# A fused attention and feed-forward kernel: scaling weight blocks in pairs, buffers per half-group, and another hand-written order

## The chip, the cores and the metric

The kernel runs on one core of a Trainium2 chip. The metric is the device time of one execution in microseconds (us), the median of several runs. The core has these engines, each with a queue of its own that it works off in order: TensorE (PE, matrix products; its weight loads are listed as PEld), VectorE (DVE), ScalarE (ACT), GpSimd (POOL) and SyncE (SP, which here only issues DMAs). An engine waits for another by semaphores. Numbers that matmuls accumulate lie in PSUM, the rest in SBUF, which has 128 partitions.

## The reference

Four batches, eight heads, 768 positions, head size 64: attention in which a position sees the 8 global positions and the 96 before it, with a linear bias, and then a feed-forward layer on its 3072 rows of 512. In short:

```python
scores = q @ k.T / 8                       # q, k, v: 4 x 8 x 768 x 64
keep = (col < n_global) | ((0 <= row - col) & (row - col < n_local))
scores = where(keep, scores - slope[head] * dist, -1e9)
a = exp(scores - max); a /= sum(a) + 1e-9
x = (a @ v) laid out as 3072 x 512
h = x @ w_in                               # w_in: 512 x 2048, float64
sp = max(h, 0) + log1p(exp(-abs(h)))
out = (h * erf(sp)) @ w_out                # w_out: 2048 x 512, float64
```

The two weight matrices come as 64-bit floats, and the kernel turns them into numbers of 16 bits itself.

## The kernel before

**Precision.** Each operand of a large matmul is held as two 16-bit halves, a high and a low one (hi, lo), and a product is three matmuls: hi by hi, hi by lo, lo by hi. So that the halves fit, a block of weights, and the values v of a batch, are first scaled by a power of two. It comes from the block's largest squared norm: matmuls of the block with itself (a gram block), the maximum of each row (`gram_max`), a matmul with a matrix of ones that sums these over partitions (`sums`), and four short DVE instructions that make the power of two and its inverse (`pow2`).

**Tiles.** The 3072 rows are 24 tiles i of 128, of which a batch b has six. Two tiles make a block u of 256 rows for the feed-forward layer. Its 2048 inner columns are two groups of 1024, so there are 24 groups n = 2u + g. The elementwise work on a group goes in two halves k of 1024 elements per partition: H holds the scaled inner values, A the tanh and its logarithm, B and C further intermediate values, g the two 16-bit halves for the second product. There are `HB` = 5 buffers for the halves of H, `CB` = 3 for A (each of a whole group), 2 each for B and C, 4 for g. The raw blocks of w_out borrow buffers of A, B, C and g before the groups need them.

**The order.** All of it is written out in a table `ORDER` of 2103 steps (line 69). The program issues the instructions of each step in turn, so every engine and the DMA queue work through their parts of the table in this order. Nothing else moves an instruction. A step is a name, its indices and often a letter for the engine (a ACT, v DVE, p POOL). Without a letter the kind has a fixed engine. The names that this text uses:

- Weights: Wd loads a block n = 0..7 of w_in, Wi Wa Wc Wb convert it from 64 bits (Wi mostly on ACT, Wc and Wb, the bitwise steps, on DVE), Wq the gram block, Wr its maximum, Wm the ones matmul, Wp the scale, Wh Wl the high and low half. Rd, Ri, Ra, Rc, Rb, Rq, Rr, Rm, Rp, Rh, Rl are the same for w_out, with 16 rows of blocks and four gram blocks. vd, vq, vm, vp load v and make its scale.
- Attention, tile i: pn a part of the penalties; TK and TQ transpose keys and queries on PE, K and Qc copy them from PSUM; S the scores of four heads on PE; E adds the bias and finds the row's least value (DVE); X the exponential (ACT); eP transposes on PE (early tiles) or et by DMA (later ones), eh and el the high and low half (a cast and a subtraction); V the weighing of the values on PE; x the division by the sums; xh, xl, xt the halves of x and their turning; vh, vl, va halves of v.
- Feed-forward, group n, half k: h the first product, H its scaled copy, t, l, i, G on ACT (tanh, two logarithms, exponential, gelu), P and Q multiplies on DVE or POOL, c and C the two combining steps on DVE, g and j the high and low half, d the second product (eight parts, 0 to 7, each six matmuls of 512 columns), O its scaled copy, o the store.

ACT holds one of two tables of functions, and `act` (line 887) loads the other one when tanh or gelu follows a logarithm or exponential, or the other way.

The lines that the change replaces in the scaling of w_in are these: one maximum per block, one scale per block.

```python
a1 = self.a1[name] = self.small.tile([P, 1], F32, tag="a1", bufs=4, name=f"a1_{name}")
...
self.pow2(f"wi{n}", to=[z[:, n : n + 1] for z in self.s_wi])
```

In the traces nearly every instruction of a step has line 195, that of the helper that records it. So rows are told apart by the names of their tiles: wo also serves as the place of raw w_in blocks, wi_hi and wi_lo are the halves of w_in, kTp and qTp transposed keys and queries in PSUM, kT and qT their copies, s scores, e exponentials, mn row minima, w and eT their halves, po the weighed values, gr_wi a gram block, a_wi its maxima, pt_wi the sums, ex_wi, swi, iwi the scale, h and H, A, B, C, g as above, o the second product's sums.

Of the kernel before, what the change touches and what calls it, by code (L numbers as in the profile page):

```python
# [11 lines left out]
F32 = mybir.dt.float32  # L12
# [9 lines left out]
P = 128  # L22
# [13 lines left out]
HB = 5  # L36
CB = 3
# [32 lines left out]
pn2v TK0 vd0,1,3 pn1a K0a Wd1 Wi0a pn5v ld1,0 KC0,0p Wa0a TQ0 Wc0 Qc0a Wb0 pn3p Wi1a S0,0 TK1 Wq0 E0,0,1 vd0,0,3  # L70
vq0,1,3 ld1,1 vd0,2,3 Wa1a Wr0v pn0p X0,0,1 Wc1 vq0,2,3 E0,0,0 Wm0 K1v vq0,0,3 Rd0 Wb1 TQ1 ld2,0 S0,2 ld0,2 Wq1 pn6a
Qc1a Wp0 ld1,2 vm0 Rd2 pn4p pn7p eP0,0,1 E0,2,1 KC0,1p X0,0,0 E0,2,0 vp0 Ri2p S1,0 eh0,0,1v eP0,0,0 Wh0a el0,0,1 vh0a
Wr1a X0,2,1 TK2 ld2,1 X0,2,0 eP0,2,1 K2a TQ2 E1,0,1 eh0,0,0a Wd2 vl0 KF3p eh0,2,1v E1,0,0 Wd3 Rd4 el0,2,1 S1,2 el0,0,0
eP0,2,0 V0,0 Wl0 ld3,0 Rd5 X1,0,1 eh0,2,0a Ri0a Ra2v E1,2,0 eP1,0,1 el0,2,0 Rd3 Wm1 Wi2v V0,2 Wd4 eh1,0,1a vh1a ld3,1
E1,2,1 Ra0v Rc2 Wa2v X1,0,0 Ri5p Ri3p eP1,0,0 Rd1 Qc2a X1,2,0 X1,2,1 x0 Rb2 Wc2 Wb2 eh1,0,0a vl1 S2,0 Wi3a Wq2 el1,0,1
Wr2v Wa3a TK3 eP1,2,0 el1,0,0 Wc3 Wi4p Wp1 Ra5a Wb3 Ra3a xP0 Ri4a vd1,0,6 Rc3 Wm2 Wa4a Wh1a Ra1a Wp2 Wq3 va1 eh1,2,0a
E2,0,1 Wr3v E2,0,0 xh0v X2,0,1 Wc4 S2,2 Rc0 xl0v eh2,0,1a Wl1 X2,0,0 el1,2,0 Wb4 eh2,0,0a eP1,2,1 ld2,2 Wq4 E2,2,1
eh1,2,1a Wm3 Rb0 Ra4a V1,0 Rd6 Wh2a el1,2,1 vh2a Rc5 K3a V1,2 el2,0,1v Rc4 Wp3 el2,0,0p Wl2 Ri1a X2,2,1 x1 Wd5 xP1
Wh3a Wi5p Ri6a Wr4v Wa5a et2,0,1 xh1a TQ3 va2 eh2,2,1a vq1,0,6 E2,2,0 Ra6a Wl3 Qc3v xl1v Rd7 Wm4 Wd7 Rc1 vd1,1,6 vl2
Rc6 Rb1 Rd12 Wc5 h0,0 h0,1 Ri7a Wd6 Rd13 Wb5 Rd14 el2,2,1p Rb6 Wp4 Rb4 Wq5 S3,0 ld3,2 et2,0,0 Ra7a H0,0a Wh4a Wl4  # L80
E3,0,1 Wr5a X2,2,0 vq1,1,6 Rb3 Ri12p h0,2 ld4,0 Wi7a vd1,2,6 E3,0,0 Ra12a Wa7v Wm5 X3,0,0 Rq0 H0,1a et2,2,1 Rd15 Rb5
# [24 lines left out]
et8,0,0 K9v H5,2v d3,1 X8,2,1 G4,0 x7 o0,1 el8,0,1p d3,2 d3,3 S9,0 xt6 eh8,2,1a et8,0,1 j3,1 d3,4 P4,0v vd2,5,6 Q4,0v
c4,0 C4,0 vl8 d3,5 xh7v el8,2,1p G4,1 d3,6 va8 t5,0 d3,7 eh8,2,0v h5,3 el8,2,0v et8,2,1 ld10,1 i4,1 g4,0a TQ10 O1,0v
E9,0,0 E9,0,1 l5,0 xl7p j4,0 H5,3v V8,0 S9,2 xt7 Qc10v X9,0,0 et8,2,0 h6,0 ld10,0 E9,2,0 vq2,5,6 i5,0 X9,0,1 eh9,0,0v
P4,1p G5,0 o1,0 ld11,1 O1,1a V8,2 Q4,1p c4,1 x8 vd3,0,6 h6,2 eh9,0,1v t5,1 d4,0 el9,0,1p xh8a C4,1 ld9,2 et9,0,1 TK10
d4,1 el9,0,0p E9,2,1 K10a g4,1p d4,2 et9,0,0 H6,0a d4,3 P5,0v xl8p h6,1 X9,2,0 X9,2,1 eh9,2,0v H6,2a Q5,0p vh9v va9  # L110
l5,1 S10,0 ld11,0 el9,2,0v eh9,2,1a vl9 E10,0,1 vq3,0,6 et9,2,0 j4,1 el9,2,1p i5,1 X10,0,1 G5,1 h6,3 V9,0 E10,0,0 TQ11
xt8 d4,4 vd3,1,6 H6,3v S10,2 H6,1v P5,1p t6,0 h7,0 h7,2 t6,1 c5,0 X10,0,0 Qc11a ld10,2 et9,2,1 vq3,1,6 eh10,0,1a
eh10,0,0a E10,2,0 l6,0 Q5,1p H7,0v C5,0 g5,0p H7,2v V9,2 el10,0,1v c5,1 E10,2,1 h7,1 vd3,2,6 l6,1 X10,2,1 i6,0 d4,5
TK11 H7,1a el10,0,0v ld12,1 et10,0,1 x9 C5,1 va10 d4,6 K11v xh9a et10,0,0 g5,1v X10,2,0 h7,3 d4,7 eh10,2,1v S11,0 o1,1
j5,0 j5,1 vq3,2,6 vm2 G6,0 el10,2,1p vh10v xl9v eh10,2,0a E11,0,1 xt9 vl10 d5,0 G6,1 el10,2,0p d5,1 d5,2 P6,0v ld11,2
# [92 lines left out]
class Kern:  # L208
# [178 lines left out]
    def wi_sums(self, n):  # L387
        self.sums(self.a1.pop(f"wi{n}"), f"wi{n}")
# [801 lines left out]
```

## Time and profile before

| | us |
|---|---|
| median of three runs (700.65 to 701.38) | 701.26 |
| the profiled execution | 701.05 |
| its span in the trace | 699.0 |
| PE busy | 656.1 |
| ACT busy | 618.2 |
| DVE busy | 598.3 |
| POOL busy | 244.9 |

The profiled execution's time is that of the whole launch; the span goes from the first instruction to the last. Busy time is what an engine spends in instructions. An engine that is not busy either waits for another one or has nothing left. A row of a time line gives, in square brackets, how long its engine was idle before it, and which engine's work ended that. Times in the trace are counted from the start of the span. The first 7 us are the set-up, which the change leaves as it is. The granted clock of PE is at its lower level, half, in some stretches before 130 us, and at its upper one from there to the end.

### The profile page before, as it was taken

Reading aid. Unit: us, or ns where it says so; the run is one execution under the profiler, and the core shown is the slowest. Engines: PE = TensorE matmul, PEld = TensorE weight load, DVE = VectorE, ACT = ScalarE, POOL = GpSimd, SP = SyncE. Lnnn points to the kernel's source line nnn. Section 1 sums busy time; section 2 is a strip of 40 time slices with the busy share of each in tenths; the row PEclk is TensorE's granted clock in tenths of the full one; section 3 lists DMA queues with packets and bytes.
Section 4 is the critical chain, followed back from the end, with each engine's and each line's share of the span. In section 5 each row is a group of like instructions: output and inputs, shape, how many; then the busy total and the mean of one; then the engine's idle time right before and its main releaser. Section 6 shows DMA issues by size and latency. Waiting matters only on the chain.

```text
span 699.0 us, 13913 instructions
## 1 busy us (share of the span) xinstructions
PE 656.1 (94%) x5280; PEld 457.0 (65%) x5280; DVE 598.3 (86%) x1104; ACT 618.2 (88%) x1004; POOL 244.9 (35%) x167
## 2 busy tenths in 40 slices
PE   3856898999999999999999999999999999999996
PEld 2645786775765785775766766776766766667552
DVE  4799889999999889897996899798877899795894
ACT  4876889999998899898999899999989799998880
POOL 3021022254532845443306323571534412425200
PEclk9975989899999999999999999999999999999999
DMA  8986966757456676434353565534445445130000
GB/s 268 272 258 189 294 180 128 153 102 122 114 84 121 152 129 128 107 74 103 87 101 76 122 137 92 136 77 91 91 92 107 91 106 116 28 57 31 0 31 35
DMA packets 201288, 81.74 MB, mean 117 GB/s; under 512 B 186748, under 2 KB 186748, under 8 KB 201212
## 3 DMA queue, kind: packets, MB, share of 16 engines
q1 hardware_dynamic: 201212, 80.77, 51.5%
q8 instruction: 43, 0.70, 0.4%
q14 instruction: 33, 0.27, 0.1%
HBM read 41.95 MB, written 6.29 MB: 69 GB/s over the span
## 4 chain that ended last, share of the span: by engine, by line
PE 44%; ACT 4%; DVE 2%; issue 1%; ACTq 0%
PE o L195 19%; PE h L195 19%; PE s L195 3%; PE po L195 2%; ACT L195 1%; ACT A L195 1%; PE qTp L195 1%; PE kTp L195 1%; ACT B L195 0%; ACT e L195 0%; DVE C L195 0%; DVE A L195 0%; DVE g L195 0%; DVE B L195 0%; ACT C L195 0%
## 5 line engine op out<-in xcount | busy, mean ns | idle before, releaser
L195 PE MATMUL h<-xT,wi_hi 128*128 128x256 f16 x1536 | 263.6, 278 | 2.4 <-DVE xT L195 1.0
L195 PE MATMUL o<-wo,g 128*128 128x512 f16 x1152 | 262.5, 379 | 0.1
L195 PE MATMUL h<-xT,wi_lo 128*128 128x256 f16 x768 | 212.8, 277 | 0.0
L195 PEld LDWEIGHTS <-g 128*128 128x128 f16 x1152 | 110.4, 98 | 121.8 <-issue 3.3
L195 PEld LDWEIGHTS <-wi_hi 128*128 128x128 f16 x1536 | 151.0, 100 | 32.2 <-issue 5.4
L195 POOL TENSOR_TENSOR w<-e,w 128x512 f16<-128x512 f32 (+1 forms) x54 | 76.2, 1414 | 154.1 <-ACT w L195 111.4
L195 ACT ACT_TABLE_LOAD x95 | 121.9, 1283 | 9.1 <-DVE wi_lo L641 7.5
L195 ACT ACTIVATE e<-e,mn 128x256 f32<-128x256 f32 (+1 forms) x192 | 91.9, 480 | 3.2 <-DVE mn L195 2.9
L195 PEld LDWEIGHTS <-wi_lo 128*128 128x128 f16 x768 | 76.4, 100 | 11.3 <-issue 1.3
L195 DVE CUSTOM_DVE_ANT_0 e<-s,pen 128x256 f32<-128x256 f32 (+1 forms) x192 | 68.2, 394 | 15.1 <-PE s L195 10.5
L195 DVE SCALAR_TENSOR_TENSOR C<-A,B 128x1024 f32<-128x1024 f32 x48 | 65.0, 1354 | 8.4 <-POOL B L195 8.1
L195 DVE SCALAR_TENSOR_TENSOR g<-C,gs,g 128x1024 f16<-128x1024 f32 x48 | 67.8, 1415 | 2.8 <-POOL g L195 1.3
L195 DVE SCALAR_TENSOR_TENSOR C<-C,H 128x1024 f32<-128x1024 f32 x48 | 61.7, 1286 | 0.5
L195 PE MATMUL s<-kT,qT 64*128 64x256 f32 (+1 forms) x384 | 57.9, 409 | 4.2 <-DVE mn L195 2.7
L195 POOL TENSOR_SCALAR g<-C,gs 128x1024 f16<-128x1024 f32 x23 | 32.2, 1398 | 84.2 <-DVE C L195 53.3
L195 POOL TENSOR_TENSOR B<-C,B 128x1024 f32<-128x1024 f32 x18 | 47.2, 2621 | 33.2 <-DVE A L195 32.7
L195 POOL TENSOR_TENSOR A<-A,B 128x1024 f32<-128x1024 f32 x15 | 37.5, 2501 | 51.8 <-ACT C L195 44.6
L195 ACT ACTIVATE A<-A,halves 128x1024 f32<-128x1024 f32 x48 | 54.8, 1142 | 0.2
L195 ACT ACTIVATE B<-A 128x1024 f32<-128x1024 f32 x48 | 50.8, 1058 | 4.7 <-DVE C L195 3.1
L195 DVE TENSOR_TENSOR A<-A,B 128x1024 f32<-128x1024 f32 x33 | 41.9, 1269 | 12.3 <-ACT C L195 7.6
L195 ACT ACTIVATE C<-A 128x1024 f32<-128x1024 f32 x48 | 50.5, 1054 | 1.5 <-DVE g L195 1.2
L195 ACT ACTIVATE A<-H 128x1024 f32<-128x1024 f32 x48 | 50.0, 1050 | 1.4 <-DVE H L195 1.0
(141 smaller groups left out, 930.8 us busy)
## 6 DMA issues: line engine op xcount, KB each, us to landing
wo<-in_moe_w_in SPq DMA_DIRECT2D x8, 1024.0 KB
raw_wo<-in_moe_w_out SPq DMA_DIRECT2D x12, 512.0 KB, 7.1
out<-osb SPq DMA_DIRECT2D x24, 256.0 KB, 2.2
kraw<-in_k SPq DMA_DIRECT2D x23, 256.0 KB, 4.6
qraw<-in_q SPq DMA_DIRECT2D x23, 256.0 KB, 3.3
vraw<-in_v SPq DMA_DIRECT2D x23, 256.0 KB, 3.0
va<-vb SPq DMA_DIRECT2D x20, 240.0 KB, 3.7
vm<-in_v SPq DMA_DIRECT2D x18, 256.0 KB, 3.0
```

The source lines that it names most:

```text
L195: i = getattr(self.engine, name)(*a, **k)
```

## The change

Four things.

1. The scale of weight blocks is made for two blocks at once. `gram_max` writes the maxima of two blocks into the two columns of one tile; the ones matmul (Wm, Rm) and the scale (Wp, Rp) then run once for a pair m, on two columns: four and two times instead of eight and four.
2. A tile of A holds half a group, and there are five of them (`CB`) instead of three whole ones. `half` returns the tile of the half. A raw row block of w_out takes one of these tiles instead of half of a whole one.
3. There are six buffers for the halves of H (`HB`) instead of five.
4. The table `ORDER` is a new one throughout (2091 steps). Some steps change engine: of the 48 P multiplies POOL has 13 where it had 15, of the 48 Q 11 where it had 18; of the low halves of the exponentials (el) 44 where it had 54; of their high halves (eh) DVE has 53 where it had 36; of the scaled copies H it has 42 where it had 49.

A step `SS` is added that the table does not use, and the branch for other sizes of n_global and n_local, which does not run here, is fitted to the pairs.

```diff
-HB = 5
-CB = 3
+HB = 6
+CB = 5
...
-pn2v TK0 vd0,1,3 pn1a K0a Wd1 Wi0a pn5v ld1,0 KC0,0p Wa0a TQ0 Wc0 Qc0a Wb0 pn3p Wi1a S0,0 TK1 Wq0 E0,0,1 vd0,0,3
...
+pn1a TK0 K0v vd0,0,3 Wi0a Wa0a TQ0 Wd1 Wc0 Wb0 pn3p Qc0v KC0,0p S0,0 ld1,0 pn2p pn0p ld1,1 pn7a Wi1a E0,0,1 ld1,2 TK1
...
     def gram_max(self, name, z="v"):
 
-        a1 = self.a1[name] = self.small.tile([P, 1], F32, tag="a1", bufs=4, name=f"a1_{name}")
+        kind, n = name[:2], int(name[2:])
+        if (kind, n // 2) not in self.a1:
+            self.a1[kind, n // 2] = self.small.tile([P, 2], F32, tag="a1", bufs=4, name=f"a1_{name}")
+        a1 = self.a1[kind, n // 2][:, n % 2 : n % 2 + 1]
...
-    def wi_sums(self, n):
-        self.sums(self.a1.pop(f"wi{n}"), f"wi{n}")
+    def wi_sums(self, m):
+        self.sums(self.a1.pop(("wi", m)), f"wi{m}")
...
-        self.pow2(f"wi{n}", to=[z[:, n : n + 1] for z in self.s_wi])
-        self.wi_done = n + 1
+        self.pow2(f"wi{m}", 2, [z[:, 2 * m : 2 * m + 2] for z in self.s_wi])
+        self.wi_done = 2 * m + 2
         self.h_scales(0)
...
-        elif b == 0 and c % 2 == 0:
-            t = self.chain.tile([P, 2, 2 * DM], F32, tag="A", bufs=self.cb, name=f"raw_wo_{n}")
-            self.raw_wo[n], self.raw_wo[n + 1] = t[:, 0:1, :], t[:, 1:2, :]
+        elif b == 0:
+            self.raw_wo[n] = self.chain.tile([P, 1, 2 * DM], F32, tag="A", bufs=self.cb, name=f"raw_wo_{n}")
...
     def half(self, n, k):
-        return self.A[n][:, k * HW : (k + 1) * HW]
+        return self.A[n, k]
 
     def tanh_part(self, n, k):
-        if k == 0:
-            self.A[n] = self.chain.tile([P, GW], F32, tag="A", bufs=self.cb, name=f"A_{n}")
+        self.A[n, k] = self.chain.tile([P, HW], F32, tag="A", bufs=self.cb, name=f"A_{n}_{k}")
         self.act(self.half(n, k), self.H[n, k], AF.Tanh, scale=0.5, g=True)
```

**What moves: DVE's first steps after the set-up.** Two penalties, the two bitwise steps of weight block 0 (wo), a bias step of two heads in two instructions each (ISA), the maximum of the gram block, a bitwise step of block 1. Before:

```order
L195 TENSOR_SCALAR pen<-wi_lo 128x384 x2
L195 SCALAR_TENSOR_TENSOR wo<-wo 128x1024 x2
L195 ISA e_0_1_203,mn_176<-s_0_1_184,pen 128x128
L195 ISA mn_176 128x1
L195 ISA e_0_1_203,mn_176<-s_0_1_184,pen 128x128
L195 ISA mn_176 128x1
L195 TENSOR_REDUCE a_wi_215<-gr_wi_194 128x1
L195 SCALAR_TENSOR_TENSOR wo<-wo 128x1024
```

After, where the key and query copies stand here too, and the maximum does not:

```order
L195 COPY kT<-kTp_153 128x4x128
L195 SCALAR_TENSOR_TENSOR wo<-wo 128x1024 x2
L195 COPY qT_175<-qTp_164 128x512
L195 ISA e_0_1_192,mn_173<-s_0_1_179,pen 128x128
L195 ISA mn_173 128x1
L195 ISA e_0_1_192,mn_173<-s_0_1_179,pen 128x128
L195 ISA mn_173 128x1
L195 SCALAR_TENSOR_TENSOR wo<-wo 128x1024
```

The copies kT and qT came from ACT, and the two penalties went to ACT and POOL.

**What moves: the scale on DVE.** Before, the scale of block 0 (ex_wi, swi, iwi) follows a bitwise step of block 1, and bias steps of the second four heads of tile 0 come after it:

```order
L195 COPY kT<-kTp_189 128x4x128
L195 SCALAR_TENSOR_TENSOR wo<-wo 128x1024
L195 TENSOR_SCALAR ex_wi_263<-pt_wi_226 128x1
L195 TENSOR_SCALAR ex_wi_263<-ex_wi_263 128x1
L195 TENSOR_SCALAR swi<-ex_wi_263 128x1
L195 TENSOR_SCALAR iwi<-ex_wi_263 128x1
L195 ISA e_2_1_279,mn_176<-s_2_1_241,pen 128x128
```

After, it is made for blocks 0 and 1 together (128x2), behind these bias steps and behind the maximum of block 1; the softmax halves of tile 0 (eT) stand behind it:

```order
L195 ISA e_2_0_275,mn_173<-s_2_0_237,pen 128x128
L195 ISA mn_173 128x1
L195 TENSOR_REDUCE a_wi_271<-gr_wi_254 128x1
L195 TENSOR_SCALAR ex_wi_293<-pt_wi_281 128x2
L195 TENSOR_SCALAR ex_wi_293<-ex_wi_293 128x2
L195 TENSOR_SCALAR swi<-ex_wi_293 128x2
L195 TENSOR_SCALAR iwi<-ex_wi_293 128x2
L195 CAST eT_0_1_307<-eP_0_1_227 128x2x128
L195 TENSOR_TENSOR eT_0_1_307<-eP_0_1_227,eT_0_1_307 128x2x128
```

So the scale now needs both maxima, and that of block 1 is on DVE just ahead of it.

**What moves: ACT's first steps.** From the copy of the first queries to block 1's conversion, the first exponentials and the sums of squares of v (vm), before:

```order
L195 COPY qT_178<-qTp_170 128x512
L195 ACTIVATE wo<-wo 128x1024
L195 ACTIVATE vm_1_158,a_v_208<-vm_1_158 128x1024
L195 ACTIVATE wo<-wo 128x1024
L195 ACT_TABLE_LOAD
L195 ACTIVATE e_0_1_203,sm_177<-e_0_1_203,mn_176 128x128 x2
L195 ACTIVATE vm_2_212,a_v_208<-vm_2_212 128x1024
L195 ACTIVATE vm_0_206,a_v_208<-vm_0_206 128x1024
L195 ACTIVATE pen<-wi_lo 128x384
L195 COPY qT_259<-qTp_233 128x512
L195 ACTIVATE e_0_0_223,sm_177<-e_0_0_223,mn_176 128x128 x2
```

After, from the first table load on:

```order
L195 ACT_TABLE_LOAD
L195 ACTIVATE e_0_1_192,sm_174<-e_0_1_192,mn_173 128x128 x2
L195 ACTIVATE vm_1_202,a_v_225<-vm_1_202 128x1024
L195 ACTIVATE pen<-wi_lo 128x384
L195 ACTIVATE e_2_1_245,sm_174<-e_2_1_245,mn_173 128x128 x2
L195 ACTIVATE e_0_0_222,sm_174<-e_0_0_222,mn_173 128x128 x2
L195 COPY qT_269<-qTp_230 128x512
L195 ACTIVATE gr_wi_210,a_wi_271<-gr_wi_210 128x256
L195 ACTIVATE vm_2_249,a_v_225<-vm_2_249 128x1024
L195 ACTIVATE vm_0_160,a_v_225<-vm_0_160 128x1024
```

The maximum of the gram block of weights 0 (gr_wi, a_wi) is now on ACT, behind six exponentials of tile 0 and the query copy of tile 1. On PE, the ones matmul of block 0 (pt_wi) that stood between the first gram block and the queries of tile 1 is gone, and a transposing of exponentials (eP) stands in its place.

## Rows read from the trace of the kernel before

**Rows 1.** The page, first part: busy us, share of the span, instructions.
```profile
PE 656.1 (94%) x5280; PEld 457.0 (65%) x5280; DVE 598.3 (86%) x1104; ACT 618.2 (88%) x1004; POOL 244.9 (35%) x167
```

**Rows 2.** Stretches: start:end, length, busy PE PEld DVE ACT POOL, PE clock, DMA share, GB/s.
```profile
28.00:60.00 32.00, 20.53 (x161) 15.55 (x159) 31.52 (x80) 23.54 (x56) 5.02 (x6) 0.76 0.73 225
60.00:140.00 80.00, 70.18 (x584) 57.11 (x585) 74.23 (x185) 69.70 (x135) 15.57 (x15) 0.82 0.77 193
140.00:215.00 75.00, 74.42 (x637) 51.36 (x635) 72.64 (x134) 74.50 (x133) 34.75 (x24) 1.00 0.56 100
215.00:690.00 475.00, 473.57 (x3825) 321.02 (x3822) 405.12 (x650) 432.26 (x647) 183.46 (x107) 1.00 0.44 91
```

**Rows 3.** DVE's time line, 7 to 28 us: start, us, operation, [idle before].
```profile
11.86 2.67 DVE L195 SCALAR_TENSOR_TENSOR wo<-wo 128x1024 int32<-128x1024 int32 x2 [3.33 <-ACT wo L195]
...
17.41 0.42 DVE L195 TENSOR_REDUCE a_wi<-gr_wi 128x1 f32<-128x256 f32 x1 [2.46 <-PE gr_wi L195]
...
22.39 0.29 DVE L195 CUSTOM_DVE_ANT_0 e<-s,pen 128x128 f32<-128x128 f32 x1 [0.76 <-PE s L195]
...
24.38 0.29 DVE L195 CUSTOM_DVE_ANT_0 e<-s,pen 128x128 f32<-128x128 f32 x1 [1.49 <-PE eP L195]
...
27.68 0.42 DVE L195 CUSTOM_DVE_ANT_0 e<-s,pen 128x256 f32<-128x256 f32 x1 [1.05 <-PE eP L195]
```

**Rows 4.** The time lines of DVE (first row) and PE around 214 us.
```profile
213.84 1.27 DVE L195 SCALAR_TENSOR_TENSOR g<-C,gs,g 128x1024 f16<-128x1024 f32 x1
...
214.94 2.32 PE L195 MATMUL o<-wo,g 128*128 128x512 f16 x10
```

**Rows 5.** The time line of ACT, 7 to 27 us.
```profile
9.67 2.16 ACT L195 ACTIVATE wo<-wo 128x1024 f32<-128x1024 f32 x2
...
14.25 1.13 ACT L195 ACTIVATE wo<-wo 128x1024 f32<-128x1024 f32 x1 [1.94 <-DMA wo<-in_moe_w_in]
...
17.46 1.28 ACT L195 ACT_TABLE_LOAD   x1
...
26.19 0.36 ACT L195 ACTIVATE gr_wi<-gr_wi 128x256 f32<-128x256 f32 x1
```

**Rows 6.** The time line of PE, 7 to 20 us.
```profile
12.36 1.23 PE L195 MATMUL s<-kT,qT 64*128 64x128 f32 x8 [1.42 <-ACT qT L195]
...
17.89 0.59 PE L195 MATMUL pt_wi<-a_wi,ones 128*128 128x1 f32 x2 [0.52 <-DVE a_wi L195]
```

**Rows 7.** DVE by shape: count | busy us, mean ns | idle before.
```profile
L195 DVE SCALAR_TENSOR_TENSOR C<-A,B 128x1024 f32<-128x1024 f32 x48 | 65.0, 1354 | 8.4 <-POOL B L195 8.1
...
L195 DVE TENSOR_SCALAR H<-h,hs 128x512 f32<-128x512 f32 x49 | 36.3, 743 | 4.6 <-PE h L195 4.6
...
L195 DVE CAST w<-e 128x512 f16<-128x512 f32 x29 | 16.5, 570 | 6.5 <-ACT e L195 6.5
...
L195 DVE COPY qT<-qTp 128x512 f32<-128x512 f32 x8 | 5.5, 682 | 0.0
...
L195 DVE TENSOR_SCALAR wo<-raw_wo,swo 128x512 f16<-128x512 f32 x5 | 2.4, 478 | 0.0
...
L195 DVE TENSOR_SCALAR ex_wi<-pt_wi 128x1 int32<-128x1 int32 x8 | 1.2, 148 | 0.0
```

**Rows 8.** The time lines of DVE (two rows) and POOL near 605 us.
```profile
604.59 2.57 DVE L195 CAST w<-e 128x512 f16<-128x512 f32 x1
607.77 0.43 DVE L195 CAST w<-e 128x512 f16<-128x512 f32 x1 [0.61 <-ACT e L195]
...
604.33 2.55 POOL L195 TENSOR_TENSOR A<-A,B 128x1024 f32<-128x1024 f32 x1 [6.07 <-ACT C L195]
```

**Rows 9.** The chain of waits, 353 to 365 us: start, us, engine, operation.
```profile
355.18 0.44 PE qTp L195 x4
...
363.30 0.70 PE po L195 x24
```

More of the change, by code (lines that the diff above doesn't have):

```diff
@@ L481, in weights @@
             self.gram_max(f"wi{n}")
-            self.wi_sums(n)
-            self.wi_scale(n)
-            for part, e in (("h", "a"), ("l", "v")):
-                self.wi_halves(n, e, part)
+            if n % 2:
+                self.wi_sums(n // 2)
+                self.wi_scale(n // 2)
+                for k in (n - 1, n):
+                    for part, e in (("h", "a"), ("l", "v")):
+                        self.wi_halves(k, e, part)
         for b in range(2 * NG):
@@ L491, in weights @@
             self.gram_max(f"wo{b}")
-            self.wo_sums(b)
-            self.wo_scale(b)
-            for n in range(b * HC, (b + 1) * HC):
-                for part, e in (("h", "a"), ("l", "v")):
-                    self.wo_split(n, e, part)
+            if b % 2:
+                self.wo_sums(b // 2)
+                self.wo_scale(b // 2)
+                for n in range((b - 1) * HC, (b + 1) * HC):
+                    for part, e in (("h", "a"), ("l", "v")):
+                        self.wo_split(n, e, part)
     def v_load(self, b, i, k):
@@ L728, in width, with score_tile, score_part @@
         return WIN if i % NT else P
-    def score_part(self, i, p):
+    def score_tile(self, i):
+        self.score_part(i, 0)
+        self.score_part(i, 2, self.ps_h, "h")
+    def score_part(self, i, p, pool=None, tag="s"):
         c, n = self.cs[i], self.width(i)
         c0 = i % KR * KP + PREV + NGL + P - n
-        pss = [self.ps_a.tile([P, 2, WIN], F32, tag="s", bufs=2, name=f"s_{i}_{p}_{j}") for j in range(2)]
+        pss = [(pool or self.ps_a).tile([P, 2, WIN], F32, tag=tag, bufs=2, name=f"s_{i}_{p}_{j}") for j in range(2)]
         for a in range(2):
@@ L1054, in branch @@
             pool = lambda n, b, **k: cx.enter_context(tc.tile_pool(name=f"{n}_{int(fast)}", bufs=b, **k))
[L1055 removed]
+            self.cb, self.hb = (CB, HB) if fast else (2, 2)
             for n in ("pt", "vs", "qT", "us", "vm", "a_v", "gr", "a1", "hs", "h_done", "raw_wo", "raws", "tp", "cs", "va", "vb", "xT", "hp", "H", "A", "B", "C", "g", "pos", "osb"):
@@ L1065, in branch @@
             if not fast:
-                with tc.tile_pool(name="wr", bufs=HC + 1) as self.wr:
+                with tc.tile_pool(name="wr", bufs=2 * HC) as self.wr:
                     self.weights()
```

245 lines of the change are left out of this document (122 added, 123 removed).

## The prediction

> **What bounds the kernel now.** I began with the busy times, then read stretches of the span, then DVE's waits in the order in which they happen. [rows 1] TensorE (PE) is busy 656.1 us of a span of 699.0 and VectorE (DVE) 598.3, so neither is slack. [rows 2] Of the 43 us that PE is idle, little lies late: from 140 to 215 it is busy 74.42 of 75, from 215 to 690 473.57 of 475. The rest lies before 140 us and in the tail. So the end is the moment at which PE has got through the opening, plus PE work that does not change.
>
> What sets that moment is mostly DVE. [rows 3] shows its five waits: 3.33, 2.46, 0.76, 1.49 and 1.05 us, 9.1 us in all, the last ending at 27.7 us. [rows 2] From 28 to 215 us DVE is busy 31.52 + 74.23 + 72.64 = 178.4 of 187: another 8.6 us of idle time, but in small holes. [rows 4] shows how close the two engines are: DVE's low half of the activations for group 3 ends at 213.84 + 1.27 = 215.11 us, and PE's ten down-projection matmuls that begin with this group start at 214.94 (the first two use the high half). PE has no gap there, DVE has none before it. So until about 215 us these two finish together, and **DVE's start plus DVE's work plus its holes up to this point is a floor under the end**. DVE has less work per group behind it (no weights are left to convert): from 215 to 690 it is busy 405 of 475 [rows 2], so it has room later, and what is left is PE's.
>
> So I compare before and after at this one point, the first down matmul of group 3, in four terms: idle time of DVE in the opening, its holes after that, DVE work ahead of the point, PE work behind it.
>
> **Term 1, DVE's opening.** I followed the new rows of DVE, ACT and PE by hand up to 41 us, with the durations of the trace.
> The key copy goes from ACT to DVE, so ACT converts weight block 0 about 0.4 us sooner: before it ends at 9.67 + 2.16 = 11.83 [rows 5], now at 11.4. DVE, done with the key copy at 8.7, waits 2.85 instead of 3.33.
> The query copy (0.68 [rows 7]) also goes to DVE, but behind both bitwise steps of block 0 (2.67 [rows 3]): it ends at 14.65, before at 12.3 on ACT. The scores (1.23 [rows 6]) follow, so the first bias step starts at 16.05: a wait of 1.4 that was not there.
> Block 1 still waits for its load, at 14.25 [rows 5]; DVE converts it to 19.9. Then it needs the second pair of scores, which on PE now stands behind a transposing that needs the first exponential. That one pays the table load of 1.28 [rows 5] and ends near 18.9; the scores end at 21.85. Wait 2.05.
> **The pair.** The scale of blocks 0 and 1 needs both maxima. That of block 1 is on DVE at 23.4 (with 0.15 of waiting). That of block 0 was DVE's first job after the gram matmuls (at 17.41 [rows 3]); now it is on ACT behind two parts of exponentials of tile 0 that wait for DVE at 22.5, and a query copy. It starts at 24.55 and takes 0.36 [rows 5]; the ones matmul takes up to 0.59 [rows 6]. The scale starts at 25.5: DVE waits 2.1. Queued behind it are the transposed softmax parts of tile 0 and the scale of v, for which ACT in turn waits until about 30.4.
> Next, the bias of tile 1 waits for scores that PE could not start before: 1.4. ACT then works off 8.4 us in a row before DVE gets its cast of tile 1: 0.35 and 1.0 lost; and a score pair behind the weighing of tile 0 costs 1.1.
> Sum: 2.85 + 1.4 + 2.05 + 0.15 + 2.1 + 1.4 + 0.35 + 1.0 + 1.1 = 12.4 us against 9.1, so **+3.3 us**. Below, it can be 0: steps of a few tenths may fall together, and before had its last wait at 27.7. Above I take 5, if what ACT owes at 39 us costs another wait of half of the largest in [rows 3].
>
> **Term 2, DVE's holes from 28 to 215 us**, 8.6 us. In a hole DVE waits for ACT, PE or POOL. If DVE comes 3.3 us later and the other engine does not, a hole shrinks by as much as it is long, up to 3.3 us in all; if the other engine was itself waiting for DVE (ACT's exponentials follow DVE's bias steps, PE's transposings follow them), nothing shrinks. From 140 to 215 ACT is busy 74.50 of 75 [rows 2], so it has no room to come earlier; from 60 to 140, where 5.8 of the 8.6 lie, it is busy 69.70 of 80 and PE 70.18, so they have. I take half: **-1.6 us**, bounds 0 and -3.3.
>
> **Term 3, DVE work ahead of group 3.** Counted in both orders. Gone or moved behind: four scalings of w_in with five short instructions and two of w_out with four, at 0.15 each, 3.0 + 1.2 = 4.2 [rows 7]; six high halves of w_out 6 x 0.48 = 2.9; four moves of H 4 x 0.74 = 3.0; one pair of the two steps on C, 1.35 [rows 7] and about the same, 2.6; smaller ones (weight conversions, two penalties, an output, a bias) 4.3. Together 17.0. Added: eleven casts of exponentials at 0.43 when free [rows 8], 4.7; three query and two key copies 5 x 0.68 = 3.4 [rows 7]; three subtractions of about the size of such a copy, 2.0, and smaller ones (integer conversions of w_out, maxima, a penalty) 5.3. Sum 15.4, net **-1.6 us**. The bounds: the 29 such casts of before took 0.570 in the mean [rows 7], which with eleven makes the net 0; -3 if half of the added ones fall into waits.
> The rule to weigh here is one of contention. The rows first: a DVE cast of 0.43 took 2.57 from 604.59, when GpSimd (POOL) was in a multiply of 2.55 from 604.33 [rows 8]. The Trainium skill, "SBUF — State Buffer", section "SBUF: two separate sides", says that the two engines share a port pair that one holds for a whole instruction while the other blocks; by that rule the trace agrees. A sum that let every added cast wait as this one did would be 11 x 2.1 = 24 us; the mean of the 29 says that few do, and the order takes multiplies off POOL (24 of 33 stay there), so I keep the mean as the bound.
>
> **Term 4, PE work.** Behind the point stand one key transposing (0.44, like the query's) and one weighing (0.70) more than before [rows 9]: **+1.1 us**. The six ones matmuls that go lie ahead of the point, under waits of DVE: nothing. The weighing waits for nothing late, so this term is firm to 0.2.
>
> **The rest.** The sixth H buffer and A in five halves take the place of five and three whole ones: 44 KB a partition either way. What they can give is bounded by what PE still loses after 140 us, 0.58 from 140 to 215 and 1.43 from 215 to 690 [rows 2]: 0 to -2.0. I take 0, since a new order brings its own pauses. Loads: SP has weight block 3 behind the low half of v of tile 0, in both orders; that is now some 3 us later, and ACT reaches it at 39.5, when it should be there: nothing, else part of term 1's upper end. The store at the end is the same.
>
> **Sum.** +3.3 - 1.6 - 1.6 + 1.1 = +1.2, on a profiled execution of 701.05 us (a span of 699.0 and 2.05 around it). The median of the three runs is 701.26, so I add there: 702.46, rounded **702.5 us**, 0.2% slower. The terms do not end low together: the holes shrink only as far as the opening is late. With an opening of 0 and no shrinking, 0 - 3 + 1.1 - 2.0 = -3.9 gives 697.4; at the upper ends, 5 + 0 + 0 + 1.1 gives 707.4.
>
> **Rivals.**
> (a) Slower: the holes do not shrink. Then +3.3 - 1.6 + 1.1 = +2.8: 704.1; at the upper ends 707.4. For it: ACT is full from 140 us on [rows 2], and before that its exponentials follow DVE's bias steps, so it is made late by the same waits. Against: PE and ACT are both idle an eighth of 60 to 140 us. It decides if, of the 8.6 us, more than 7 are still there in the profile after.
> (b) Faster: DVE opens no later than before, since waits that I added one after the other overlap, and the buffers take away PE's late pauses: -1.6 + 1.1 - 2.0 = -2.5, 698.8. For it: DVE has 26 steps up to the second bitwise step of block 2 where it had 35, so less stands in front; the late pauses exist. Against: the pair's scale cannot start before ACT's maximum, and ahead of 215 us no buffer is shown to be waited for.
> (c) Slower still, by ACT and DVE in turn. If ACT falls behind in the opening, DVE's multiplies wait for ACT's logs and ACT's logs for B buffers that DVE frees; every exchange carries the lateness on and adds its own latency. At two waits of about 1.5, as the fourth of [rows 3], on top of (a), the end is 707. It decides if DVE's idle time from 60 to 215 us, 8.1 of the 8.6 before, grows by 3.
> (d) The casts behind POOL: four of eleven at 2.1 more is 8.6 us on DVE and 711, and the contention above is its mechanism. The mean of [rows 7] speaks against it.
> That the change does not do what it says (halves of A freed apart, scales in pairs) is ruled out by the rows of the order. That it buys and costs nothing is the lower half of the forecast.
>
> **How the numbers follow.** The forecast, with 700.0 to 704.0 as its own range, 0.42; (a) 0.23; (b) 0.22; (c) 0.09; (d) 0.04. A difference under 0.2% (1.4 us, 699.9 to 702.7) is about what a measurement of this kernel can tell from none. Of the forecast 0.22 lies within it and 0.20 above; (a) to 0.03 within, all the rest of it, (c) and (d) above; (b) to 0.17 below and 0.05 within. So faster 0.17, same 0.30, slower 0.53. The range that leaves out 2 in 10 goes from 697.4, the sum of the low ends, to 707.4, that of the high ones.
>
> **What would show it.** Right: in the profile after, DVE's waits up to 41 us sum to about 12 us, one of some 2 us before the scale of the first pair (ended by the ones matmul), and the holes after that to about 7; the first down matmul of group 3 starts between 215 and 216. Wrong in term 1: that sum is under 10. Wrong in term 2: the holes are as large as before. Wrong in term 3: the casts' mean is far from 0.5. Wrong as a whole: PE pauses for more than 3 us in sum after 220 us; then the floor that I used is not what decides.

## The result, and the profile after

The changed kernel takes 705.28 us (median of five executions: four from 702.69 to 707.19; the fifth, 717.62, was disturbed and is left out of the ratio), against 701.25: the ratio is **1.0058, 95% interval 1.003 to 1.0087**, slower by 0.58%. The profiled execution is the fastest of them, 702.69 us with a span of 700.9.

The page of after, busy time as in [rows 1]: PE 7.6 us less, DVE 19.7 more, POOL 43.1 less.

```profile
PE 648.5 (93%) x5268; PEld 450.8 (64%) x5268; DVE 618.0 (88%) x1118; ACT 612.2 (87%) x985; POOL 201.8 (29%) x143
```

The stretches of after, columns as in [rows 2]:

```profile
28.00:60.00 32.00, 17.75 (x144) 14.07 (x144) 29.26 (x67) 26.11 (x55) 5.73 (x5) 0.71 0.82 255
60.00:140.00 80.00, 65.37 (x578) 53.59 (x579) 76.80 (x173) 66.20 (x135) 17.98 (x16) 0.82 0.74 175
140.00:215.00 75.00, 74.21 (x615) 50.64 (x613) 73.95 (x140) 73.86 (x124) 24.85 (x19) 1.00 0.58 114
215.00:690.00 475.00, 474.27 (x3844) 321.63 (x3841) 422.25 (x685) 429.64 (x640) 147.38 (x87) 1.00 0.43 89
```

From 215 to 690 us PE is as full as before (474.27 of 475), though DVE has 17 us more to do there: that work costs PE no pause.

DVE's waits in after, as in [rows 3]:

```profile
11.35 2.49 DVE L195 SCALAR_TENSOR_TENSOR wo<-wo 128x1024 int32<-128x1024 int32 x2 [2.72 <-ACT wo L195]
...
15.76 0.29 DVE L195 CUSTOM_DVE_ANT_0 e<-s,pen 128x128 f32<-128x128 f32 x1 [1.33 <-PE s L195]
...
20.43 0.29 DVE L195 CUSTOM_DVE_ANT_0 e<-s,pen 128x128 f32<-128x128 f32 x1 [0.86 <-ACT pen L195]
...
23.75 0.16 DVE L195 TENSOR_SCALAR ex_wi<-pt_wi 128x2 int32<-128x2 int32 x1 [2.03 <-PE pt_wi L195]
...
26.38 0.42 DVE L195 CUSTOM_DVE_ANT_0 e<-s,pen 128x256 f32<-128x256 f32 x1 [1.20 <-ACT vm L195]
...
37.45 0.69 DVE L195 TENSOR_TENSOR eT<-eP,eT 128x512 f16<-128x512 f32 x1 [1.14 <-ACT eT L195]
39.43 0.42 DVE L195 CUSTOM_DVE_ANT_0 e<-s,pen 128x256 f32<-128x256 f32 x1 [1.29 <-PE s L195]
```

These are the waits that the prediction walked through, in its order: 2.72 (2.85 was forecast), 1.33 (1.4), 0.86 (2.05), 2.03 for the ones matmul of the pair (2.1), 1.20 (1.4), 1.14 and 1.29. Their sum is 10.6, not 12.4. Two ended otherwise than forecast: this trace puts the 0.86 and the 1.20 down to ACT (a penalty, a sum of squares), where the prediction had scores on PE. The low half for group 3 ended at 215.06, where before had 215.11 [rows 4]:

```profile
213.78 1.28 DVE L195 SCALAR_TENSOR_TENSOR g<-C,gs,g 128x1024 f16<-128x1024 f32 x1
```

In this one execution, then, nothing was lost up to the point, and the 1.6 us by which it is longer than the profiled one of before lie behind it. But the median is 2.6 us above this one. Where that goes is seen in a second trace.

### The profile page after: what moved, and what is told of

It reads as the page before. It is cut to its first block, busy times and chain, and to the rows that moved or that the text cites. A ratio compares the mean times of both kernels' runs of the same rounds, so it can differ in the third digit from the quotient of the medians.

```text
span 700.9 us, 13820 instructions
## 1 busy us (share of the span) xinstructions
PE 648.5 (93%) x5268; PEld 450.8 (64%) x5268; DVE 618.0 (88%) x1118; ACT 612.2 (87%) x985; POOL 201.8 (29%) x143
## 4 chain that ended last, share of the span: by engine, by line
PE 74%; DVE 16%; ACT 4%; issue 2%; DMA 1%; SPq 1%; DVEq 0%; ACTq 0%
PE h L195 31%; PE o L195 30%; PE s L195 5%; PE po L195 4%; DVE wo L195 3%; DVE C L195 2%; DVE raw_wo L195 2%; DVE e L195 2%; DVE w L195 1%; PE kTp L195 1%; DVE g L195 1%; PE qTp L195 1%; DMA qraw<-in_q 1%; DVE A L195 1%; DVE B L195 1%
## 5 line engine op out<-in xcount | busy, mean ns | idle before, releaser
L195 PE MATMUL h<-xT,wi_hi 128*128 128x256 f16 x1536 | 259.1, 275 | 0.0
L195 POOL TENSOR_TENSOR w<-e,w 128x512 f16<-128x512 f32 (+1 forms) x44 | 65.9, 1502 | 167.4 <-DVE w L195 77.8
L195 POOL TENSOR_SCALAR g<-C,gs 128x1024 f16<-128x1024 f32 x20 | 28.7, 1437 | 142.5 <-DVE C L195 64.4
L195 DVE SCALAR_TENSOR_TENSOR C<-A,B 128x1024 f32<-128x1024 f32 x48 | 61.0, 1273 | 0.3
L195 DVE TENSOR_TENSOR A<-A,B 128x1024 f32<-128x1024 f32 x35 | 46.3, 1323 | 6.4 <-ACT C L195 5.1
L195 PEld LDWEIGHTS s<-kT,qT 64*128 64x128 f32 x384 | 35.5, 199 | 25.3 <-issue 9.9
L195 DVE TENSOR_TENSOR B<-C,B 128x1024 f32<-128x1024 f32 x37 | 48.3, 1306 | 3.7 <-POOL A L195 3.3
L195 ACT ACTIVATE B<-B 128x1024 f32<-128x1024 f32 x48 | 50.4, 1052 | 0.4
```

The source lines that it names most:

```text
L195: i = getattr(self.engine, name)(*a, **k)
```

## Experiments

All ratios are to the kernel before on the same chip. Its median was 700.6 to 701.5 there, with single executions from 697.6 to 704.1, so a single trace says little on the total, and much on durations and waits. The rows come from several chips, so they are compared by their ratios rather than by their medians.

| kernel | median, us | ratio, 95% interval |
|---|---|---|
| after, again | 706.00 | 1.0057 (1.0037 to 1.0077) |
| new opening, old rest | 707.96 | 1.0085 (1.0066 to 1.0104) |
| old opening, new rest | 705.46 | 1.0049 (1.0032 to 1.0066) |
| before, A in six halves | 700.79 | 0.9998 (0.9982 to 1.0015) |
| before, DVE late | 704.08 | 1.0057 (1.0035 to 1.0078) |
| before, 36 POOL multiplies | 705.19 | 1.0069 (1.0043 to 1.0095) |
| before, 72 POOL fills | 700.26 | 0.9983 (0.9966 to 1.0001) |
| after, maximum 0 on DVE | 703.58 | 1.0047 (1.0030 to 1.0064) |
| after, load of block 1 first | 703.39 | 1.0052 (1.0030 to 1.0073) |
| after, both of these | 702.51 | 1.0037 (1.0020 to 1.0053) |
| before, load of block 1 first | 698.18 | 0.9966 (0.9952 to 0.9981) |
| after, 15 steps from POOL to ACT | 708.34 | 1.0117 (1.0098 to 1.0136) |

**The changed kernel again** (no edit).

> The changed kernel once more, to see whether its times scatter wider than those of the kernel before (702.7 to 707.2 in four executions, against 700.2 to 701.4). Theory T (a floor set by the opening of VectorE, then TensorE work): the scatter is chance of a few executions, and the median falls near 703, +0.3%. Rival S (something in the new order is sensitive to a quantity that differs from one execution to the next): the median stays near 705, +0.5%, executions lie 3 us and more apart, and a profiled execution differs from the first one (span 700.9) in one stretch.

Rival S on the median: 706.0, though before scatters as widely on this chip. The trace (span 702.8) differs from the first in the opening. The time line of ACT of the first, then of the second, where the first weight block that comes by a later load (block 1) is waited for:

```profile
13.99 2.16 ACT L195 ACTIVATE wo<-wo 128x1024 f32<-128x1024 f32 x2 [2.26 <-DMA wo<-in_moe_w_in]
```

```profile
15.14 2.16 ACT L195 ACTIVATE wo<-wo 128x1024 f32<-128x1024 f32 x2 [3.27 <-DMA wo<-in_moe_w_in]
```

And DVE's time line of the second, three of its eight waits:

```profile
17.34 1.23 DVE L195 SCALAR_TENSOR_TENSOR wo<-wo 128x1024 int32<-128x1024 int32 x1 [0.92 <-ACT wo L195]
...
22.60 0.29 DVE L195 CUSTOM_DVE_ANT_0 e<-s,pen 128x128 f32<-128x128 f32 x1 [1.88 <-PE s L195]
...
29.61 0.43 DVE L195 CUSTOM_DVE_ANT_0 e<-s,pen 128x256 f32<-128x256 f32 x1 [2.07 <-PE s L195]
```

Block 1 landed 1.15 us later, and DVE waited 0.92 for its conversion. The next two waits shown, 0.86 and 1.20 in the first trace, are 1.88 and 2.07. Here are the rows of PE ahead of the first of these, in the first trace, then in the second:

```profile
18.97 0.60 PE L195 MATMUL qTp<-ident,qraw 128*128 128x128 f32 x4
19.50 0.71 PE L195 MATMUL s<-kT,qT 64*128 64x128 f32 x8
```

```profile
20.23 1.06 PE L195 MATMUL qTp<-ident,qraw 128*128 128x128 f32 x4
21.22 1.23 PE L195 MATMUL s<-kT,qT 64*128 64x128 f32 x8
```

The same transposings and scores took 1.0 us longer together, and that is about what the wait grew by. PE's granted clock is on record at its upper level from 17.8 to 24.6 us in the first trace (it fell behind a pause of PE of 2.1 us), and from 29.7 on in the second. Ahead of its rise PE worked without a pause from 14.49 to 17.67 in the first, and paused for 0.45 at 15.86 in the second, for a load. But in a later kernel (after, load of block 1 first) it worked without a pause from 14.71 on, and the upper level is on record from 21.0 only; what decides the moment stays open.

The sum up to 43 us is 13.1, and 13.9 in a third trace of this opening (the next kernel; upper level from 28.7). So 10.6, 13.1 and 13.9, mean 12.5; three traces of the old opening have 9.1, 10.0 and 8.6, mean 9.2.

**New opening with the old rest, and the other way.** The two orders are joined at the first down matmul of group 3. The first kernel has the table of after up to the step d3,0 and then what is left of the steps of before, in the order of before. The second has it the other way round, with A in six halves and H in five buffers.

> The new order up to the first down matmul of group 3 (about 215 us), then the remaining steps in the order of before, with the new kernel's buffers and paired scales. Theory T: that matmul starts at about 215, as in both profiles, and the rest is that of before: 701 to 702, +0.1%. Rival S1 (the scatter arises in the opening, ahead of 215 us): executions 3 us and more apart and a median of 704 to 705. Rival S2 (it arises behind): a tight set near 701.5.

> The order and the scaling of before up to the first down matmul of group 3, then the remaining steps in the new order (A in six half tiles and H in five, since that opening needs them). Theory T: what stands behind the point costs 1.1 to 1.4 us more on TensorE in the new order, so 702.4 to 702.7, +0.2%. Rival S1 (the scatter arises in the opening): a tight set at 702.5 or below. Rival S2: executions 3 us and more apart, median near 705.

Both medians missed theory T, to the slow side; the executions of the second lie within 1.8 us, as S1 has it. The joints have a price of their own: with the old opening the point is reached at 214.8 us, as before, and the last down matmuls start 480.9 us behind it instead of 477.0. Of these 3.9 us, 2.2 are pauses of TensorE between 230 and 245 us; the new rest finds steps done in another order there, and five H buffers instead of six, and which of the two makes the pauses was not tested. So these two don't say what the rest costs. What they give are two more traces of each opening: by the time of the point, the scatter lies ahead of it (S1), since in the unjoined traces the last down matmuls start 478.5 and 478.3 us behind it in after, 477.0 and 477.1 in before and its next variant. That is 1.3 us more in after.

**Before with A in halves.**

```diff
-CB = 3    # whole tiles of A
+CB = 6    # half tiles of A
-        return self.A[n][:, k * HW : (k + 1) * HW]
+        return self.A[n, k]
```

> The kernel before with one edit: each tile of A holds half a group and there are six of them in place of three whole ones, so that halves come free apart; order, scaling and H buffers as before. Theory T: no buffer of A is waited for where it counts, 701.3, within 0.1%. Rival B (the late pauses of TensorE, 0.7 us at 350 to 360 and 0.6 at 530 to 540, are waits for buffers): 699.5 to 700.5, -0.15 to -0.25%.

Theory T: 0.9998, and its trace has both late pauses of PE as before (0.74 and 0.66). They are no waits for A. A sixth H buffer was not tested by itself.

**Before with DVE late.**

```diff
-... Rd0 Wb1 TQ1 ld2,0 S0,2 ...
+... Rd0 Wb1 ZZ12 TQ1 ld2,0 S0,2 ...
```

The step ZZ12 is twelve DVE instructions on a scratch tile of 200 columns.

> The kernel before with twelve short extra VectorE instructions on a scratch tile behind the second bitwise step of weight block 1 (about 21 us), some 3 us in all: only this engine's opening is made late, nothing else changes. The holes of term 2 tell the theories apart. Theory T (half of a late opening is absorbed in later holes, as term 2 has it): the first down matmul of group 3 comes 1.5 us later and the end too: 702.8. Rival F (the waits of the opening are passed on in full): 3 us later, 704.3. Rival N (VectorE's start is no floor): under 0.5 us, 701.5.

The time line of DVE shows that the twelve took more than planned:

```profile
22.06 4.77 DVE L195 SCALAR_TENSOR_TENSOR scr<-scr 128x200 f32<-128x200 f32 x12
...
28.28 0.29 DVE L195 CUSTOM_DVE_ANT_0 e<-s,pen 128x128 f32<-128x128 f32 x1 [0.53 <-PE eP L195]
```

4.77 us were put in, and up to the point DVE is busy 4.1 us more than in the mean of the old opening. The waits of the opening took back 0.8 (8.4 in sum against 9.2), and the idle time from there to the point is 0.3 less. The point came at 217.0, 3.0 later than the mean of 214.9, 214.8 and 212.4. Of these 3.0, 0.6 stood ahead of the twelve: in this trace the wait for the gram block was 3.46 against 2.8 in the mean, so 2.4 are left to them. The median is 3.3 higher (4.0 by the ratio). With what was really put in, T has 2.4 and F 4.8, so neither holds as it stands: **between half and five sixths of a late VectorE is passed on; what is taken back is taken back in the waits of the opening, and the later holes, of which term 2 spoke, shrink by 0.3 us.**

**Before with more work on POOL.** In the three traces of the new opening I took each DVE instruction ahead of 215 us and compared it with the usual length of its shape (the tenth percentile over all traces). Those that are longer by over 0.1 us sum to 9.4, 8.4 and 7.6 us; with the old opening to 6.2, 5.4 and 5.7. Each one of them lies beside an instruction of POOL. The time line of DVE of after shows two of them, at 56.03 and 94.78, and the same two shapes at their usual length, at 94.18 and 54.84:

```profile
54.84 1.28 DVE L195 SCALAR_TENSOR_TENSOR wi_lo<-wo,swi,wi_hi 128x1024 f16<-128x1024 f32 x1
56.03 1.66 DVE L195 SCALAR_TENSOR_TENSOR raw_wo<-raw_wo 128x512 int32<-128x512 int32 x1
...
94.18 0.69 DVE L195 SCALAR_TENSOR_TENSOR raw_wo<-raw_wo 128x512 int32<-128x512 int32 x1
94.78 2.19 DVE L195 SCALAR_TENSOR_TENSOR wi_lo<-wo,swi,wi_hi 128x1024 f16<-128x1024 f32 x1
```

And POOL's time line of the same kernel:

```profile
55.81 1.32 POOL L195 TENSOR_TENSOR w<-e,w 128x512 f16<-128x512 f32 x1 [13.32 <-ACT w L195]
...
94.23 1.66 POOL L195 TENSOR_TENSOR w<-e,w 128x512 f16<-128x512 f32 x1 [14.86 <-ACT w L195]
95.86 2.44 POOL L195 TENSOR_SCALAR wo<-wo 128x512 f32<-128x512 f32 x2
```

A bitwise step of 0.69 takes 1.66, from 56.03: POOL's subtraction ends at 57.13, 1.10 after its start, and it is 0.97 late. Two kernels tell whether that is the cause, and what about POOL's work:

```diff
-... Ri5p Ri3p eP1,0,0 Rd1 ...
+... Ri5p Ri3p ZZ3 eP1,0,0 Rd1 ...
```

The step ZZ3, at twelve places, is three POOL multiplies of 200 columns on a scratch tile.

> The kernel before with 36 short extra GpSimd multiplies on a scratch tile, in twelve groups of three behind its steps between 30 and 115 us; no other engine reads them. In the traces of the changed kernel VectorE's instructions ahead of group 3 are longer by 2 us in sum than in those of before, and each long one lies beside one of GpSimd. Theory C (GpSimd's instructions hold VectorE's up): VectorE's busy time from 28 to 140 us grows by 3 us or more, single instructions by up to the length of a group, and the end comes 2 to 4 us later, 703.5 to 705.5. Rival N (the two only lie beside each other by chance): busy time and end as before, within 0.5 us.

```diff
-            self.nc.gpsimd.tensor_tensor(self.scr, self.scr, self.scr, op=ALU.mult)
+            self.nc.gpsimd.memset(self.scr, 0.0)
```

Here each place has six of them instead of three.

> As the run with 36 extra GpSimd multiplies (end 4.4 us later, the multiplies at 0.51 us when free), but with 72 extra GpSimd fills of the same scratch tile with zeros (0.27 us each), six behind each of the same steps: about as much GpSimd time, of instructions that write and read nothing. It tells what about a GpSimd instruction holds VectorE up. Theory R (an instruction that reads its input from the same memory, as the Trainium skill, page "SBUF - State Buffer", section "SBUF: two separate sides", has it for two-input instructions of VectorE): VectorE's two-input instructions keep their length, and the end is within 1 us of that of before, 700.5 to 701.7. Rival C (any GpSimd instruction): busy time of VectorE from 28 to 140 us grows by 2 or more, 703 to 705.5.

The stretches up to the end of DVE's low half for group 3 (columns as in [rows 2], the third busy time is DVE's), of before, of the one with multiplies, and of the one with fills:

```profile
0.00:215.11 215.11, 179.17 (x1445) 134.63 (x1446) 192.52 (x455) 185.41 (x357) 61.49 (x60) 0.90 0.72 177
```

```profile
0.00:218.78 218.78, 179.62 (x1446) 134.84 (x1446) 197.90 (x455) 186.19 (x357) 92.01 (x97) 0.88 0.70 174
```

```profile
0.00:215.17 215.17, 179.31 (x1445) 134.75 (x1446) 192.47 (x455) 185.91 (x357) 80.87 (x133) 0.90 0.72 177
```

Theory C for the multiplies: DVE has the same instructions and is busy 197.90 instead of 192.52; its over-long ones sum to 11.6; the end is 4.4 us later. Theory R for the fills: 19.4 us more of POOL, DVE at 192.47, the sum 5.7, no difference in time. **So it is POOL's instructions with an input in SBUF that hold VectorE up; the fills, which have none, don't.** Counted over thirteen traces (all but that of the fills), whole spans, instructions that lay beside POOL's for over 0.15 us: of those with all inputs in SBUF, 379 of 793 of the five big multiplies were longer by over 0.1 us; of those with an input in PSUM (bias steps, copies of H, of queries and of outputs, divisions) none of 1769. Who began first decides: of the 793, 454 began while an instruction of POOL was running, and the 379 are all among these; of the 339 beside which POOL's began later, none was longer. The Trainium skill, "SBUF — State Buffer", section "SBUF: two separate sides", has the exclusive port pair only for VectorE's instructions with two SBUF inputs or in a fast mode, and against two inputs only for GpSimd instructions that read SBUF; by these counts, these traces agree.

**After without the wait for the maximum of block 0.**

```diff
-... X0,0,1 E0,0,0 vq0,1,3 ... Qc1a Wr0a Rd2 E0,2,0 ...
+... X0,0,1 E0,0,0 Wr0v vq0,1,3 ... Qc1a Rd2 E0,2,0 ...
```

> The changed kernel with one step moved: the maximum of the gram block of weights 0 is taken by VectorE behind the first half of the bias of tile 0 instead of by ScalarE behind six exponentials, so the pair's scale waits for one maximum only. Theory T: the wait of 2.0 to 2.2 us ahead of the scale of the first pair shrinks to about 0.7, VectorE has 0.4 more to do, and the end comes about 1 us earlier than that of the changed kernel, 704.3 to 705. Rival N (the next wait takes it up): no change, 705.3 to 706.

DVE's time line, the scale of the pair:

```profile
22.79 0.16 DVE L195 TENSOR_SCALAR ex_wi<-pt_wi 128x2 int32<-128x2 int32 x1 [0.48 <-PE pt_wi L195]
```

The wait is 0.48 instead of 2.0 to 2.2: theory T for the wait. For the time it isn't clear of noise: by the ratios the kernel is 0.7 to 0.8 us faster than after, and the intervals overlap.

**The load of block 1 first**, in after and in before.

```diff
-pn1a TK0 K0v vd0,0,3 Wi0a Wa0a TQ0 Wd1 ... S0,0 ld1,0 pn2p ...
+pn1a TK0 K0v Wi0a Wa0a TQ0 Wd1 ... S0,0 ld1,0 vd0,0,3 pn2p ...
```

> The changed kernel with one load moved: the first 512 KB of v are loaded behind weight block 1 and the first keys of tile 1 instead of ahead of them. In three traces of that opening weight block 1 landed at 13.99, 14.49 and 15.14 us, and the sum of VectorE's waits up to 43 us was 10.6, 13.9 and 13.1. Theory L (the landing of block 1 is what lets that opening vary): it lands about 1 us sooner, and the end comes 1 to 2 us earlier, 703.5 to 705. Rival N (ScalarE and TensorE set it all the same): no change, 705.3 to 706.

> The changed kernel with both moves of the opening: weight block 1 and the first keys of tile 1 are loaded ahead of the first 512 KB of v, and the maximum of gram block 0 is on VectorE. Each alone gave 703.4 to 703.6 against 705.3 to 706.0. Theory T (the waits of the opening are passed on, and these two stand in a row): VectorE's waits up to 43 us sum to about 9, the end is at 702 to 702.8. Rival N (both take away the same wait): 703.3 to 703.8.

> The kernel before with the same load moved: weight block 1 and the first keys of tile 1 ahead of the first 512 KB of v, and the sum of squares of that part of v behind block 1's second conversion on ScalarE. Theory T: block 1 lands at about 12.6 instead of 14.3 to 15.0, VectorE's second wait (2.5 to 3.3 us for the gram block) shrinks by about 1, and the end is about 1 us earlier than that of the kernel before: 699.8 to 700.3. Rival N (later waits take it up): 700.8 to 701.3.

In before the edit moves two steps, the load (vd0,1,3) and, on ACT, the sum of squares of that part of v (vq0,1,3), which needs this load:

```diff
-pn2v TK0 vd0,1,3 pn1a K0a Wd1 Wi0a pn5v ld1,0 KC0,0p ... vd0,0,3 vq0,1,3 ld1,1 vd0,2,3 Wa1a Wr0v ...
+pn2v TK0 pn1a K0a Wd1 Wi0a pn5v ld1,0 vd0,1,3 KC0,0p ... vd0,0,3 ld1,1 vd0,2,3 Wa1a vq0,1,3 Wr0v ...
```

ACT's time line of after with the load first, and DVE's time line of before with it:

```profile
12.56 2.17 ACT L195 ACTIVATE wo<-wo 128x1024 f32<-128x1024 f32 x2 [0.62 <-DMA wo<-in_moe_w_in]
```

```profile
15.72 0.42 DVE L195 TENSOR_REDUCE a_wi<-gr_wi 128x1 f32<-128x256 f32 x1 [0.78 <-PE gr_wi L195]
```

512 KB less ahead of it let block 1 land at 12.56 instead of 13.99 to 15.14: theory L for the load. In after the gain in time isn't clear of noise: by the ratios 0.4 us with the load first and 1.4 with both moves, and their intervals overlap that of after. The trace of both has 7.6 us of waits up to 43 us, less than forecast. In before the gain is clear: the wait for the gram block falls from 2.46 [rows 3] to 0.78, the waits after it by another 1.3, and the time by 0.34%, more than T expected: **698.18 us, ratio 0.9966 (0.9952 to 0.9981), the fastest kernel of this study**.

The gram block that DVE waits for is that of weight block 0, which doesn't need block 1. What it stood behind on PE, in before, then in this kernel:

```profile
15.36 1.09 PE L195 MATMUL kTp<-ident,kraw 128*128 128x128 f32 x4 [1.78 <-DMA kraw<-in_k]
```

```profile
13.60 1.09 PE L195 MATMUL kTp<-ident,kraw 128*128 128x128 f32 x4
```

The transposing of the first keys of tile 1 waited 1.78 us for their load, which was queued behind the same 512 KB of v, and now it waits for none. So for this wait it is the keys that came sooner, and not block 1, though T had that. What the step on ACT is worth by itself was not run.

**After with fifteen steps from POOL to ACT.**

```diff
-... Ri5p ... Rh10p ... Rh14p ...
+... Ri5a ... Rh10a ... Rh14a ...
```

> The changed kernel with fifteen steps on w_out ahead of group 3 (seven conversions, eight high halves) on ScalarE instead of GpSimd, at the same places of the order. Theory C (GpSimd's instructions hold VectorE's up): what VectorE's instructions ahead of 215 us take beyond their usual length, 7.1 to 9.0 us in three traces of this order, falls by 3 or more. ScalarE, idle 20 of the 112 us from 28 to 140, takes some 10 more; if that fits, the end is 2 us earlier, 703 to 704. Rival A (ScalarE becomes the late engine): the excess falls and the end is no earlier, 705 to 709. Rival N: the excess stays above 7.

Rival A. The stretch up to the end of DVE's low half for group 3, now at 220.69:

```profile
0.00:220.69 220.69, 171.56 (x1404) 128.43 (x1405) 192.11 (x434) 190.24 (x360) 36.93 (x41) 0.89 0.71 176
```

and the same stretch of after:

```profile
0.00:215.05 215.05, 169.31 (x1404) 127.05 (x1405) 194.97 (x434) 181.96 (x345) 54.47 (x56) 0.88 0.73 181
```

With the same instructions, DVE's over-long ones fall to 5.7 us and its busy time to 192.11 (194.3 in the mean of three traces): in the changed kernel too, less work on POOL makes DVE's instructions shorter. But ACT goes from 181.96 to 190.24, and DVE waits for it: 28.6 us of idle time in that stretch, against 20.1, 23.1 and 25.8 in the three traces of the new opening. Work can't be taken off POOL for nothing here.

## Why the prediction was right and where it was not

The direction and the range were right: 705.28 lies in 697.4 to 707.4. The forecast of 702.5 was 2.8 too low, outside its own range of 700.0 to 704.0; rival (a), 704.1, was nearest. Term by term, means over three traces of each opening (the windows up to the end of DVE's low half for group 3). Single traces of one opening lie up to 3.3 us apart in a term, so the split is good to about a microsecond:

| term | predicted | measured |
|---|---|---|
| 1. waits of DVE's opening | +3.3 | +3.3 (9.2 to 12.5) |
| 2. holes after it (without the 4.5 us of set-up) | -1.6 | -2.3 (8.3 to 6.0) |
| 3. DVE work ahead of the point | -1.6 | +2.0 (192.2 to 194.3) |
| 4. behind the point | +1.1 | +1.3 |
| sum | +1.2 | +4.3 |

- **Term 1** came out at its number, in part by luck. The 12.5 is the mean of 10.6, with PE at its upper clock from 17.8 to 24.6 us, and of 13.1 and 13.9, with the upper clock on record from 29.7 and 28.7; the prediction had walked with the long scores (1.23 [rows 6]). Most places held: the wait for the pair's maximum was forecast as 2.1 and is 2.0 to 2.2. A wait for block 1's conversion, which it didn't have, is 0.37 and 0.92 in two of the three traces. Moving the maximum took 1.5 to 1.7 us off its wait, and what that gave back in time isn't clear of noise. What the pairs are worth by themselves, without the new order, was not run.
- **Term 2** came out near its number, but its reason fell. DVE made late on purpose kept its later holes but for 0.3 us. The new order has fewer of them for other reasons, which stay open.
- **Term 3** is the step that failed, by 3.6 us, beyond its upper bound of 0. 2.7 of it is contention with POOL (over-long instructions go from 5.8 to 8.5 us). I had the mechanism, and rival (d) rested on it, but I sized it by the mean of one shape, the cast of exponentials, and only for added casts. The casts were not what was hit: ahead of the point it is bitwise steps, low halves and multiplies, 0.7 to 1.3 us long, that now lie beside POOL's work. That POOL has less to do in sum (201.8 against 244.9) did not help: what counts is which DVE instruction its work lies beside. The casts' mean, its sign for a miss, is 0.59 over the span, and the ten casts of 512 columns ahead of the point took 0.41 to 0.42 each in the first trace: rival (d) fell, and the sign looked at the wrong instructions. The other 0.9 is in part my count: by the shapes ahead of the point in the two profiles, at their usual lengths, the net is -1.1, with ten casts added and not eleven. The rest stays open.
- **Term 4** held to 0.2 in its sum, with two parts that were not forecast and cancel: from the point to the last down matmuls PE is busy 1.9 us more, and not 1.1, and idle 0.8 us instead of 1.4, since the pause of 0.74 us near 351 us is gone. The halves of A alone bought nothing (0.9998), as taken; whether the sixth H buffer or the new order takes that pause away stays open.
- **Rival (b)** fell: DVE opened later, and no late pause was a wait for A. **Rival (c)**, exchanges of lateness between ACT and DVE, is not seen: DVE's idle time from 60 to 215 us is 4.3 to 6.4 in three traces where it was 6.7 to 8.1. **Rival (a)** was nearest in time, and right in that a late DVE hardly shrinks the holes; its own mark, over 7 us of idle time left from 28 to 215, gives 7.0, 8.7 and 11.4, but 2.4 to 5.4 of these are waits of the opening.
- What would show it: waits up to 41 us of "about 12", 10.6 in the first trace and 12.5 in the mean; the point at 215 to 216: 215.1 in the first trace and 217.2 in the second. PE pauses for 0.8 us in sum after 220 us, and not for 3: the floor that the prediction used stands.

## What to carry to other kernels

Where two engines share the lead, follow the new order by hand up to the last wait of the opening: most waits came out within a few tenths. Of 4.8 us put in there, between half and five sixths arrived at the end; of 3.1 us taken out, by the load moved in before, 2.4 did. Look at PE's clock in the trace that the lengths come from: the same scores took 0.71 or 1.23 us. When a change reorders steps, price contention by pairs: for each VectorE instruction with all its inputs in SBUF ask whether a GpSimd instruction that reads SBUF is now running when it starts. And the loads that the opening waits for go to the head of the queue, also those that reach the slowest engine by way of another one: moving one load behind them, with the step that needs it, was worth 0.34% here.

## What was not expected of the hardware

- GpSimd's fills cost VectorE nothing (DVE 192.47 us, before 192.52), its multiplies 0.18 us for each us (5.4 us for the 30.5 that POOL was busy longer).
- ScalarE's wait for the same 1 MB load ended between 13.99 and 15.14 us in traces of the new order, and between 14.25 and 15.17 with the old, as long as 512 KB of v stood ahead of it.
- TensorE's upper clock is first on record from 17.8 us on in one execution of the changed kernel and from 29.7 on in another, and the same eight score matmuls took 0.71 and 1.23 us. In the second, whose load was 1.15 us later too, the division of tile 0 came 3.0 us later (44.4 and 47.4).
